# The heads' normalizer: from products with a repeated identity column to a round trip through DRAM

## The chip, the cores and the metric

The kernel runs on one core of a Trainium2 chip. The metric is device time in microseconds of one execution. The median of three runs of the kernel before is 684.15 us (682.97 to 684.3). Line numbers (L624 and so on) are those of the kernel before. TensorE is called PE, VectorE DVE, ScalarE ACT, GpSimd POOL and SyncE SP, as in the profile; SP issues nearly all DMA transfers here, ACT a few.

## The reference

2048 tokens of 640 features are normalized; one branch is a linear attention with 32 heads of 20 features and a learned feature map, the other a two-layer MLP with GELU whose output gates the first.

```python
pq = jnp.einsum("bhsd,hdf->bhsf", q, w_phi)
pk = jnp.einsum("bhsd,hdf->bhsf", k, w_phi)
phi_q = jnp.concatenate([_softmax(pq, axis=-1), _softmax(-pq, axis=-1)], axis=-1)
phi_k = jnp.concatenate([_softmax(pk, axis=-1), _softmax(-pk, axis=-1)], axis=-1)
kv = jnp.einsum("bhsf,bhsd->bhfd", phi_k, v)
z  = jnp.einsum("bhsf->bhf", phi_k)
num = jnp.einsum("bhqf,bhfd->bhqd", phi_q, kv)
den = jnp.einsum("bhqf,bhf->bhq", phi_q, z)[..., None] + 1e-6
o = num / den
...
return x + s * g      # s = o @ wo, g = silu(mlp(xn))
```

The change is about `z`: for each head, the sum of the key features over all tokens, 32 x 40 = 1280 numbers. Every token's query features are multiplied by it to get `den`.

## The kernel before

The work is in four stages.

1. Start, to about 30 us: weights are loaded, the feature map is folded into the key and query weights, tokens are normalized.
2. Projections, to about 251 us: for each of 16 token tiles of 128, keys, values and queries are projected on PE (L332). Key features are accumulated with the values into one PSUM bank `kv` by `kv_acc` (L403). The value tile carries a column of ones per head, so that each head's sum of key features falls out as one more row. The query features, not normalized yet, go to DRAM as `e_dram`, from ACT's queue (L385, L909, L911).
3. The MLP, about 251 to 555 us: twelve units, two halves of the tokens times six groups of two hidden tiles. A unit makes seven products of the first layer (`part`, L650), sums them on DVE, applies GELU on ACT (`act`, L655, L657), makes the low parts of the hidden tiles on DVE (`act_lo`, L661), and multiplies by the second layer (`down`, L679, 30 matmuls for each of the two outputs o = 0 and o = 1, each in groups of three, one and one PSUM banks); DVE adds the result to `y` (L686, L688). `down` loops over the two hidden tiles outside and over the output banks of the group inside. For o = 0 it takes the hidden tiles h11 and h21, for o = 1 h12 and h22.
4. Output, to the end: products with the state of the heads (L769, L780, L787) and with `wo` (L844), stores of the output.

In stage 3 every engine takes its instructions in the order of the code (`manual_schedule`), so the order written in the loop over units is the order of each queue, SP's too. An engine that waits holds up all that stands behind it.

Between the stages `kv_rest` (L597) copies the bank `kv` into the SBUF tile `kvr` with three ACT copies (L603); POOL clears the columns that are not used (L600, L601). In `kvr` the heads lie in groups of three: row 32e + 20 of `kvr` has the sums of group 4g + e at columns 120g to 120g + 119, for e = 0 to 3 and g = 0 to 2.

`kv_norm` (L620) spreads these four rows onto all 128 partitions. It is called once, in unit 0, after the first layer's products of that unit and ahead of its `down` (L942). For each e it takes one column of the identity, repeated 128 times, as the one operand and all of `kvr` as the other, so that each row of the product is row 32e + 20; ACT then copies the product from PSUM into the tile `zrep` (L627, L630), in the order of the heads. `zrep` is one of 23 slabs, tiles of 5120 B in each partition, that most large tiles of the kernel share; so are `eq`, `ez`, `hs`, `w1s`, `w2s`, `xhi` and `y`.

The readers of `zrep` are the sixteen products of `q_norm` (L725) on POOL: `ez` is the query features `eq` of a token tile times `zrep`. The rest of `q_norm` sums, divides and stores the normalized query features to `phi_dram`. The first `q_norm` (token tile 8) begins with unit 1, ahead of the rounding of that unit's w2 weights, whose low parts POOL makes too (L148).

On SP the order around the call is: unit 0's loads of w1 and w2 (`raw`, L154), of `xhi` and `xlo` (L699, L700) and of `eq` for tile 8 (L719); then what `kv_norm` issues, which is nothing in the kernel before; then unit 1's four loads `raw`, its `xhi`, `xlo` and its `eq` loads; then the stores of unit 0's `xhi` and `xlo` (L712, L713). The w1 weights that unit 0 loads are turned into sums and differences by POOL (L415), rounded by ACT (L426), and their low parts made by POOL (L427), within unit 0; unit 1 uses them. Those that unit 1 loads are for unit 2, and so on.

A transfer of the kind that the change brings in is used once elsewhere: `pair_stats` stores the mean and the reciprocal deviation of 256 tokens to `st_dram` (L293) and loads them back, repeated on all partitions, into `bc` (L295).

Of the kernel before, what the change touches and what calls it, by code (L numbers as in the profile page):

```python
# [8 lines left out]
F32 = mybir.dt.float32  # L9
F32R = mybir.dt.float32r  # L10
AF = mybir.ActivationFunctionType
# [3 lines left out]
S, D, H, DH, F = 2048, 640, 32, 20, 1536  # L15
P = 128
# [30 lines left out]
def hedgehog_gated_mlp_kernel(ctx: ExitStack, tc: tile.TileContext, x, xt_in, wqk, bd, wv, wo, w1, b1, w2, b2, out_t):  # L47
    nc = tc.nc
# [4 lines left out]
    dram = ctx.enter_context(tc.tile_pool(name="dram", bufs=1, space=bass.MemoryType.DRAM))  # L53
# [27 lines left out]
    def slab(dt, name, shape=(P, 2, D)):  # L81
        return slabs.tile(list(shape), dt, tag="S", name=name)
# [7 lines left out]
    def bankB(name="pB"):  # L90
        return pools["B"].tile([P, 512], F32, tag="B", name=name)
# [4 lines left out]
    xd_dram = dram.tile([P, 9, 2, CW], F32, name="xd_dram")  # L96
    w1_dram = dram.tile([NG, P, 2, 2048], F32, name="w1_dram")
    g_dram = dram.tile([KC, P, 2, CW], F32, name="g_dram")
    st_dram = dram.tile([NT // 2, 2, P, 2], F32, name="st_dram")

    ident = const.tile([P, P], F32, name="ident")
# [495 lines left out]
    def kv_rest():  # L597
        kv_acc(NT - 1, phis.pop(NT - 1), vs.pop(NT - 1))
        kvr = const.tile([P, 360], F32, name="kvr")
        nc.gpsimd.memset(kvr[64:96, 320:360], 0.0)  # L600
        nc.gpsimd.memset(kvr[96:, 240:360], 0.0)  # L601
        for p, a, b in ((P, 0, 240), (96, 240, 320), (64, 320, 360)):
            nc.scalar.activation(kvr[:p, a:b], kvp[0][:p, a:b], AF.Copy)  # L603
        return kvr


    def kv_state(kvr):
# [8 lines left out]
        for r in range(3):  # L616
            nc.vector.tensor_tensor(bdl[:80, 40 * r:40 * r + 40].rearrange("p (h d) -> p h d", d=20),
                                    ps[:80, None, 320:340].to_broadcast([80, 2, 20]),
                                    mask[:80, :2, None].to_broadcast([80, 2, 20]), op=OP.mult)
    def kv_norm(kvr):  # L620
        zf = slab(F32, "zrep")[:].rearrange("p a b -> p (a b)")
        for e, n in enumerate((360, 360, 320, 240)):
            ps = bankB()
            nc.tensor.matmul(ps[:, :n], ident[:, 32 * e + 20:32 * e + 21].to_broadcast([P, P]), kvr[:, :n],  # L624
                             start=True, stop=True)
            m = n // 120
            nc.scalar.activation(zf[:, :960].rearrange("p (g r) -> p g r", r=480)[:, :, 120 * e:120 * e + 120],  # L627
                                 ps[:, :240].rearrange("p (g r) -> p g r", r=120), AF.Copy)
            if n > 240:
                nc.scalar.activation(zf[:, 960 + 120 * e:720 + 120 * e + n], ps[:, 240:n], AF.Copy)  # L630
        return zf


# [220 lines left out]
    zf, none = None, iter(())  # L854
# [6 lines left out]
    kvr = kv_rest()  # L861
# [8 lines left out]
    for unit in range(units):  # L870
        h, g = divmod(unit, NG)
# [69 lines left out]
        if unit == 0:  # L941
            zf = kv_norm(kvr)  # L942
# [146 lines left out]
```

## Time and profile before

| What | Value |
|---|---|
| Median of three runs | 684.15 us (682.97 to 684.3) |
| Profiled execution: span from the first to the last instruction | 681.1 us |
| Granted TensorE clock over the span (mean) | 1.000 |
| PE busy, stretch of units 0 (251.5 to 279.5 us) | 28.0 us of 28.0 |
| DVE, ACT, POOL busy in the same stretch | 19.2, 16.2, 19.7 us |
| L624, products of `kv_norm` on PE | 8 matmuls, 263.6 to 265.9 us |
| L627 and L630, copies of `kv_norm` on ACT | 7, the first at 267.13, the last at 268.30 us |
| First reading of `zrep` on POOL | 279.08 us |

The page gives the span of the profiled execution and not its whole time; the runs are timed apart from it. PE's busy time is a sum of modelled spans; its rate is better read from how many matmuls fall into a stretch of the chain. Rows of the timeline have the start, the duration, the engine, the line and operation, the tiles (out<-in) and, in brackets, how long the engine was idle before and what ended that. A q after the engine's name is its queue: SPq rows are transfers issued by SP, with the time that the issue took, waits within a group of them included. A row of waits has who waited, for what, the sum in us, how often, and the longest.

### The profile page before, as it was taken

The page shows a single profiled execution, that of the slowest core. Times are in us where ns is not written, and L with a number is a line of the kernel's source. Part 1 is how long each engine was busy: PE and PEld are TensorE (multiplying, and loading weights), DVE is VectorE, ACT ScalarE, POOL GpSimd, SP SyncE. Part 2 cuts the span into 40 slices and gives each one's busy share as a digit, 9 for nine tenths or more (in the row PEclk, how much of TensorE's full clock was granted, in tenths as well). Part 3 has the DMA queues.
Part 4 walks back from the last instruction along what each step waited for, and adds up shares of the span by engine and source line. Part 5 has one row for each costly group of instructions (what it writes and reads, how often), then busy time and mean ns, then how long its engine had stood idle before and what let it go on. Part 6 is the DMA issues. An engine that isn't in the chain of part 4 may idle for free.

```text
span 681.1 us, 11991 instructions
## 1 busy us (share of the span) xinstructions
PE 676.4 (99%) x4727; PEld 592.0 (87%) x4727; DVE 454.8 (67%) x729; ACT 253.0 (37%) x400; POOL 382.2 (56%) x351
## 2 busy tenths in 40 slices
PE   9999999999999999999999999999999999999998
PEld 9999999999999998888888888888888887777876
DVE  5786665887876466586978784576876655774232
ACT  3523214333223337144254247533133254425440
POOL 3653254757767375857978952726446640783221
PEclk9999999999999999999999999999999999999999
DMA  8820144633451333329688696476363491888423
GB/s 330 311 80 1 11 142 100 227 93 137 69 200 60 115 138 135 117 88 348 209 273 278 237 426 280 129 259 224 139 216 137 151 398 47 321 296 291 150 94 109
DMA packets 73966, 125.42 MB, mean 184 GB/s; under 512 B 5822, under 2 KB 42686, under 8 KB 73014
## 3 DMA queue, kind: packets, MB, share of 16 engines
q1 hardware_dynamic: 71606, 114.17, 49.3%
q10 hardware_dynamic: 2304, 10.49, 4.4%
q8 instruction: 37, 0.61, 0.4%
q14 instruction: 19, 0.16, 0.1%
HBM read 79.54 MB, written 45.10 MB: 183 GB/s over the span
## 4 chain that ended last, share of the span: by engine, by line
PE 96%; DVE 1%; POOL 1%; issue 1%; ACT 0%; POOLq 0%
PE pA L332 30%; PE pB L679 24%; PE pB L650 22%; PE pB L844 11%; PE pB L780 3%; PE pB L769 2%; PE kv L403 2%; PE pA L173 1%; POOL wv L148 1%; PE pA L466 1%; PE pA L318 1%; PE pB L787 1%; DVE st L197 0%; DVE wk L184 0%; PE pB L624 0%
## 5 line engine op out<-in xcount | busy, mean ns | idle before, releaser
L679 PE MATMUL pB<-hs,w2s 128*128 128x512 f32 x720 | 167.1, 390 | 0.0
L679 PEld LDWEIGHTS pB<-hs,w2s 128*128 128x128 f32 x720 | 134.6, 188 | 29.4 <-PE pB L780 0.8
L650 PE MATMUL pB<-xp,w1s 128*128 128x512 f32 x324 | 81.4, 390 | 0.0
L650 PE MATMUL pB<-xd,w1s 128*128 128x512 f32 x324 | 79.3, 389 | 0.0
L358 ACT ACTIVATE e<-e 128x1280 f32<-128x1280 f32 x32 | 40.7, 1272 | 90.1 <-POOL e L353 89.5
L844 PE MATMUL pB<-oT,wo 128*128 128x512 f32 (+2 forms) x315 | 73.9, 386 | 0.0
L688 DVE TENSOR_TENSOR y<-pB,y 128x512 f32<-128x512 f32 x100 | 63.9, 680 | 12.4 <-PE pB L679 12.2
L650 PEld LDWEIGHTS pB<-xp,w1s 128*128 128x128 f32 x324 | 60.7, 188 | 12.9 <-DVE pB L925 0.4
L650 PEld LDWEIGHTS pB<-xd,w1s 128*128 128x128 f32 x324 | 60.8, 188 | 12.6
L844 PEld LDWEIGHTS pB<-oT,wo 128*128 128x128 f32 x315 | 57.1, 188 | 14.2 <-ACT ph L772 1.2
L371 POOL TENSOR_TENSOR e<-e,rc 128x1280 f32<-128x1280 f32 x16 | 39.0, 2438 | 48.8 <-DVE rc L391 48.4
L371 POOL TENSOR_TENSOR eq<-eq,rc 128x1280 f32<-128x1280 f32 x16 | 37.9, 2369 | 50.2 <-DVE rc L738 50.2
L353 POOL TENSOR_TENSOR e<-nr,e 128x640 f32<-128x640 f32 x32 | 45.5, 1424 | 30.1 <-DVE nr L352 27.7
L332 PE MATMUL pA<-wv,xp 128*128 128x320 f32 x384 | 60.7, 311 | 0.3 <-POOL wv L148 0.3
L655 ACT ACTIVATE pB<-pB,b1t 128x512 f32<-128x512 f32 x48 | 31.8, 662 | 77.2 <-DVE pB L925 27.6
L332 PE MATMUL pA<-wk,xp 128*128 128x320 f32 x384 | 59.9, 311 | 0.0
L332 PE MATMUL pA<-wq,xp 128*128 128x320 f32 x384 | 59.0, 309 | 0.0
L332 PEld LDWEIGHTS pA<-wv,xp 128*128 128x128 f32 x384 | 56.9, 188 | 0.6 <-POOL wv L148 0.5
L332 PEld LDWEIGHTS pA<-wq,xp 128*128 128x128 f32 x384 | 56.9, 188 | 0.1
L332 PEld LDWEIGHTS pA<-wk,xp 128*128 128x128 f32 x384 | 56.8, 188 | 0.1
L725 POOL TENSOR_TENSOR ez<-eq,zrep 128x1280 f32<-128x1280 f32 x16 | 47.3, 2959 | 0.2 <-PE pB L780 0.2
L427 POOL TENSOR_TENSOR w1s<-raw,w1s 128x640 fp32r<-128x640 f32 (+1 forms) x18 | 25.7, 1428 | 36.4 <-ACT w1s L426 29.2
(145 smaller groups left out, 1053.3 us busy)
## 6 DMA issues: line engine op xcount, KB each, us to landing
raw<-in_w_dram SPq DMA_DIRECT2D x42, 320.0 KB, 4.7
e_dram<-e ACTq DMA_DIRECT2D x16, 640.0 KB, 3.8
eq<-e_dram SPq DMA_DIRECT2D x16, 640.0 KB, 6.6
phi_dram<-eq SPq DMA_DIRECT2D x16, 640.0 KB, 3.5
phi<-phi_dram SPq DMA_DIRECT2D x16, 640.0 KB, 9.0
xt<-in_x_dram SPq DMA_DIRECT2D x16, 320.0 KB, 5.7
xres<-in_xt_dram SPq DMA_DIRECT2D x20, 256.0 KB, 4.3
out_dram<-xres SPq DMA_DIRECT2D x18, 256.0 KB, 3.0
```

The source lines that it names most:

```text
L332: nc.tensor.matmul(ps[:, hf, :HALF], stat_x(q, o, k, a), ws[k][:, b, hf * HALF:(hf + 1) * HALF], start=n == 0, stop=n == 3 * KC - 1)
L353: nc.gpsimd.tensor_tensor(e5[:, :, :, 1, :], nr[:, :, :, None].to_broadcast([P, 2, 16, DH]), e5[:, :, :, 0, :], op=OP.subtract)
L358: nc.scalar.activation(ef, ef, AF.Exp)
L371: nc.gpsimd.tensor_tensor(e3, e3, rc[:, :, None].to_broadcast([P, 64, DH]), op=OP.mult)
L427: nc.gpsimd.tensor_tensor(sl[:, 1, :n], src, sl[:, 0, :n].bitcast(F32), op=OP.subtract)
L650: nc.tensor.matmul(bank[ch][:], tl[:, a, off + wo_:off + wo_ + P], mov(blk, b), start=new and n == 0, stop=n == len(mms) - 1, skip_group_c ...
L655: nc.scalar.activation(ps, ps, AF.Gelu_apprx_tanh, bias=b1t[:, f:f + 1])
L679: nc.tensor.matmul(ps[:], ws[i][:, b, d * P:(d + 1) * P], hs[o][i][:, a, :], start=i == n == 0, stop=(i, n) == (GF - 1, 2), skip_group_che ...
L688: nc.vector.tensor_tensor(y, ps[:], y, op=OP.add)
L725: nc.gpsimd.tensor_tensor(zv, ef, zf, op=OP.mult)
L780: nc.tensor.matmul(po[64 * e:64 * e + 64, :256], bdk[:n, 2 * j + e, :], ph[:n, e * 256:(e + 1) * 256], start=True, stop=True)
L844: nc.tensor.matmul(ps[:, mv], w, o[:, mv], start=n == 0, stop=n == 15, skip_group_check=True)
```

## The change

The four products and the seven ACT copies go. In their place SP issues six transfers: five stores from `kvr` to a new DRAM tensor `z_dram` and one load that repeats its 1280 numbers on all 128 partitions into the slab. Four stores take one row of `kvr` each, as pieces of 120 numbers that go to every fourth place of 120 in `z_dram`; the fifth takes the 80 numbers of the last group. The load reads what the stores write, so it waits for all five. The place of the call, the readers and the form of `zrep` stay as they are.

```diff
+    z_dram = dram.tile([1440], F32, name="z_dram")
...
     def kv_norm(kvr):
+        zv = z_dram.rearrange("(g e r) -> e g r", e=4, r=120)
+        for e, m in enumerate((3, 3, 2, 2)):
+            nc.sync.dma_start(zv[e:e + 1, :m], kvr[32 * e + 20:32 * e + 21, :120 * m].rearrange("p (g r) -> p g r", r=120))
+        nc.sync.dma_start(z_dram[1200:2 * D].unsqueeze(0), kvr[84:85, 240:320])
         zf = slab(F32, "zrep")[:].rearrange("p a b -> p (a b)")
-        for e, n in enumerate((360, 360, 320, 240)):
-            ps = bankB()
-            nc.tensor.matmul(ps[:, :n], ident[:, 32 * e + 20:32 * e + 21].to_broadcast([P, P]), kvr[:, :n],
-                             start=True, stop=True)
-            m = n // 120
-            nc.scalar.activation(zf[:, :960].rearrange("p (g r) -> p g r", r=480)[:, :, 120 * e:120 * e + 120],
-                                 ps[:, :240].rearrange("p (g r) -> p g r", r=120), AF.Copy)
-            if n > 240:
-                nc.scalar.activation(zf[:, 960 + 120 * e:720 + 120 * e + n], ps[:, 240:n], AF.Copy)
+        nc.sync.dma_start(zf, z_dram[:2 * D].partition_broadcast(P))
         return zf
```

## The prediction

> **What bounds the kernel now.** I read the page first, for the busy shares and the chain that ended last, then what TensorE waited for over the whole run, then its chain in the stretch around the change.
>
> ```profile
> span 681.1 us, 11991 instructions
> PE 676.4 (99%) x4727; PEld 592.0 (87%) x4727; DVE 454.8 (67%) x729; ACT 253.0 (37%) x400; POOL 382.2 (56%) x351
> PE 96%; DVE 1%; POOL 1%; issue 1%; ACT 0%; POOLq 0%
> ```
>
> ```profile
> PE pA L466 <- PEq L1079: 0.8, 1, 0.8
> PE pA L332 <- POOL wv L148: 0.3, 1, 0.3
> PE pA L318 <- DVE xt L213: 0.2, 1, 0.2
> ```
>
> ```profile
> 251.49 12.26 PE pB L650 x54
> 263.75 2.15 PE pB L624 x8
> 265.90 13.63 PE pB L679 x60
> 279.54 12.24 PE pB L650 x54
> 291.78 13.60 PE pB L679 x60
> ```
>
> The reader is to see three things. The list of PE's waits holds three entries, 1.3 us together, all at lines of the first phase, and the chain is 96% PE: every microsecond of matmul on it is a microsecond of time. In the chain one piece begins where the other ends (251.49 + 12.26 = 263.75, + 2.15 = 265.90). And the pace is that of streaming, not of waiting: 13.60/60 and 12.24/54 are both 0.227 us per matmul, in a unit with the changed code before it and in one without. The eight matmuls of L624 (four calls, two hardware passes each) sit in this row with 2.15 us and nothing beside them.
>
> **Removed: four products, 2.15 us of PE.** Without them the first matmul of the second layer (L679) could start at 263.75. Whether it may is a question of its inputs. The first nine matmuls use the hidden tile h11 alone, the next nine h21, because the loop over the two weight tiles is outside that over the three outputs.
>
> ```profile
> 262.36 0.68 DVE L661 TENSOR_TENSOR hs<-pB,hs 128x512 fp32r<-128x512 f32 x1
> ...
> 264.62 0.69 DVE L661 TENSOR_TENSOR hs<-pB,hs 128x512 fp32r<-128x512 f32 x1 [0.49 <-ACT hs L657]
> ```
>
> The code makes the low parts in the order h11, h22, h21, so these are the first and the third: h11's is there at 263.04, h21's at 264.62 + 0.69 = 265.31. Nine matmuls from 263.75 take 9 x 0.227 = 2.04 us, so h21 is asked for at 265.79: 0.48 us after it is there. The last hidden tile, h12, is read only by the other half of the tokens, 30 matmuls (6.8 us) further on. The four PSUM banks that the products took fall away too, and unit 1 goes from L650 to L679 without a gap (291.78) with no products between. So the whole 2.15 us leaves the chain at this point.
>
> **Removed: seven ACT copies.**
>
> ```profile
> 267.13 0.37 ACT L627 ACTIVATE zrep<-pB 128x240 f32<-128x240 f32 x1
> 268.55 0.81 ACT L426 ACTIVATE w1s<-raw 128x640 fp32r<-128x640 f32 x1
> ```
>
> From 267.13 to 268.55, 1.42 us, they hold up the rounding of unit 1's weights. ACT is waited for by POOL there (below), so POOL's run begins 1.42 us sooner, while PE comes 2.15 us sooner: POOL loses 0.73 us of its lead.
>
> **Added: five stores, one load and their waits, all on SP.** The order on SP is the order of the code; the new six stand behind eq (t = 8) and ahead of unit 1's four raw loads.
>
> ```profile
> 236.25 2.04 SPq L719 DMA_DIRECT2D eq<-e_dram  x1
> 247.33 11.64 SPq L154 DMA_DIRECT2D raw<-in_w_dram  x4
> 272.09 0.53 SPq L699 DMA_DIRECT2D xhi<-xp_dram  x1
> 295.53 0.57 SPq L712 DMA_DIRECT2D xd_dram<-xhi  x1
> 296.93 0.54 SPq L713 DMA_DIRECT2D xd_dram<-xlo  x1
> ```
>
> ```profile
> 251.72 0.55 ACT L603 ACTIVATE kvr<-kv 128x240 f32<-128x240 f32 x3
> 255.94 0.19 POOL L601 MEMSET kvr<- 32x120 f32 x1
> ```
>
> SP is free at 236.25 + 2.04 = 238.3 and must wait for kvr: until ACT's copies end at 252.27, or until POOL's clearing ends at 256.13 if the stores are held for that as well (they do not read those columns). I take the later one. The trace has no store of one partition's row; the nearest is the store of the layer norm's statistics with the repeating load that waits for it:
>
> ```profile
> 177.90 0.37 SPq L293 DMA_DIRECT2D st_dram<-pst  x1
> 182.62 0.34 SPq L295 DMA_DIRECT2D bc<-st_dram  x1
> bc<-st_dram SPq DMA_DIRECT2D x4, 256.0 KB, 5.7
> eq<-e_dram SPq DMA_DIRECT2D x16, 640.0 KB, 6.6
> ```
>
> An issue is 0.37 us and the dependent load follows 182.62 - 177.90 - 0.37 = 4.35 us later. Five issues (1.85) and one such round trip: SP issues the load at 256.13 + 1.85 + 4.35 = 262.3 (258.5 by the early end). The load repeats one row of 5120 B onto 128 partitions, 640 KB. From below it costs 5.7 us, the 256 KB that L295 repeats in the same way; from above 2.5 times that for 2.5 times the bytes, 14.3. I take 6.6, the load with the same bytes and the same rows in SBUF, which differs only in that its source rows are not one row. So the normalizer lands at 268.9, and between 264.2 and 276.6.
>
> **Who waits for it.** The first reader is POOL's product ez (L725) of unit 1, and behind it on POOL stand the low halves of unit 1's w2 tiles (L148) that PE needs at 291.78.
>
> ```profile
> 269.44 1.58 POOL L427 TENSOR_TENSOR w1s<-raw,w1s 128x640 fp32r<-128x640 f32 x1 [8.01 <-ACT w1s L426]
> 279.08 2.96 POOL L725 TENSOR_TENSOR ez<-eq,zrep 128x1280 f32<-128x1280 f32 x1
> 282.00 3.08 POOL L148 TENSOR_TENSOR w2s<-raw,w2s 128x640 fp32r<-128x640 f32 x2
> 287.78 0.74 POOL L415 TENSOR_TENSOR st<-raw 128x256 f32<-128x256 f32 x1 [2.70 <-PE pB L650]
> ```
>
> POOL works without a break from 269.44 into ez, so it comes to ez at 279.08 - 1.42 = 277.66. Up to there a landing costs nothing, and both bounds lie before it. PE is hit only later: it wants the first low half after one matmul of L679, at 291.78 - 2.15 + 0.23 = 289.86; ez (2.96) and half of 3.08 go before, so a landing after 289.86 - 4.50 = **285.36** stalls PE, one for one. Margin 16.5 us on my value, 8.8 on the worst. The cover is POOL's own run; without it the whole wait would be paid.
>
> Behind the new waits on SP stand the four raw loads. They go out by about 264 instead of 247.33 to 259. POOL reads the first at L415, at 287.78 - 2.15 = 285.6, and itself waited for PE there, not for a load. Four loads of 320 KB are two of 640 KB, 2 x 6.6 = 13.2 us even one after the other: they are in by 282.1 if the normalizer lands at 268.9, by 289.8 if at 276.6. Even then POOL makes unit 2's forms in four steps like L415 and some four like L427, 4 x 0.74 + 4 x 1.58 = 9.3 us, by 299.1, and PE wants them at 291.78 + 13.60 - 2.15 = 303.2. I cost it at nothing. xhi, which follows, was held until 272.09 by a slab that PE's L679 frees:
>
> ```profile
> SPq L699 <- PE pB L679: 9.0, 1, 9.0
> SPq L713 <- DVE xlo L710: 0.7, 1, 0.7
> ```
>
> so SP has time to spare up to there. The normalizer's own tile takes its place in the pool of slabs some 5 us earlier (262.3 against 267.13); if it had to wait as xhi did, until 272.09, it would land at 278.7 (286.4 by the upper bound): a loss of 0 to 1.0 us.
>
> **The sum.** -2.15 (PE) + 0 (ACT, POOL, SP, the load) = -2.15 us; the span 681.1 becomes 678.95. The page gives no time of the whole execution beside its span; the median of the runs, 684.15, is 3.05 above it, and I keep that difference: **682.0 us**, 0.31% less. From L679 of unit 0 on, PE waits for nothing in the list above, so the gain travels to the end.
>
> **The rivals.**
> *The late normalizer (slower).* If each of the five stores waits for the one before, because their targets in DRAM are interleaved, SP pays 5 x 4.72 (177.90 to 182.62) = 23.6 us and issues the load at 279.7; it lands at 286.3 by the 640 KB row, 285.4 and 294.0 by the bounds. PE stalls 0.05 to 8.7 us: 682.0 to 690.6, with 685 in the region of a landing at 288.4. It decides from a landing of 285.36 on, and from 287.5 the kernel is slower than before. Against it: L712 and L713 above write interleaved stretches of one DRAM tensor, and the second goes out 1.40 us after the first and was held only 0.7 us, by DVE, though such a store takes longer to land:
>
> ```profile
> xd_dram<-xhi SPq DMA_DIRECT2D x4, 576.0 KB, 3.5
> ```
>
> For it: the views of z are three-level and different in the fifth store, and a single-partition store is nowhere in this trace. The Trainium skill, page "DMA: Bandwidth & Descriptors", section "Anatomy of one DMA", puts a transfer at about 2.0 us plus its bytes at 436 GB/s and lays the fixed part to the confirmation of the write; by that even the stores one after the other would cost some 10 us and the load 3.5, an estimate that lands before 277.66 and costs nothing. The 4.35 us of the row above is twice that page's figure, so the rows count.
>
> *No gain at this place.* PE has its 2.15 us less of products but waits for the hidden tiles: if h21's low part were needed from the first matmul, L679 would start at 265.31 instead of 265.90, a gain of 0.59, 683.6 us. For it: DVE's third L661 ends only 1.56 us after 263.75. Against it: the order of the loop, and the 0.48 us of lead. The same size would come from slabs given out in another order, so that a tile of a later unit waits as xhi does; every such wait lies on SP now, and none is on PE.
>
> **How the numbers follow.** The forecast 72%, no gain 12%, late normalizer 16%. Under 0.2%, 1.37 us, a measurement of this kernel cannot be told from no change (its three runs lie 1.33 apart). The forecast is faster; no gain is "same"; of the late landings, spread evenly over 285.4 to 294.0, a tenth is faster (stall under 0.78), three tenths same (under 3.52), six tenths slower. Faster 0.72 + 0.01 = 0.73, same 0.12 + 0.05 = 0.17, slower 0.10. The range: from the lowest run before less 2.15 and a little for the runs, 682.97 - 2.15 - 0.2 = 680.6, up to 685.0, which takes in all of "no gain" and the late landings up to 288.4; the forecast's own is 680.8 to 682.8.
>
> **What would show it.** Right: L679 of unit 0 follows L650 with no gap and no row of L624; PE's waits still sum to 1.3 us; ez of unit 1 starts near 277.7 and is released by POOL's own order; the load of z goes out at 258 to 263 and lands before 277; the five stores leave within 2.5 us; ACT's L426 starts at 267.1. Wrong: a wait of POOL for the load at ez, a wait of PE for POOL's L148 at the second layer of unit 1, stores about 4.7 us apart on SP, PE waiting for DVE's L661 at 263.75, or a new PE wait after 305 that eats the 2.15.

## The result and the profile after

The changed kernel takes 681.8 us in the median of eight runs, beside 683.65 us of the kernel before: a ratio of 0.9973, with a 95% interval of 0.9963 to 0.9983. A second set of runs gave 681.13 beside 683.23 us, 0.9971 (0.996 to 0.9981). The forecast was 682.0. The profiled execution has a span of 679.2 us and a time of 680.95, near the lower end of the eight (680.72 to 683.57).

The chain that ended last, around unit 0, of the changed kernel (start, duration, piece; the lines of the MLP are now L647 and L676):

```profile
251.64 12.27 PE pB L647 x54
263.90 13.60 PE pB L676 x60
277.50 12.24 PE pB L647 x54
289.74 13.60 PE pB L676 x60
303.34 12.24 PE pB L647 x54
```

From the first matmul of the MLP to the first of the second layer there are now 12.26 us, where there were 14.41: the 2.15 us of the products are out and nothing stands in their place. They stay out: the last long piece of PE, 112 matmuls with `wo`, begins at 652.68 instead of 654.71, and the MLP itself had begun 0.15 us later here, which makes 2.18 us between the two points.

The issues of SP around the call:

```profile
252.45 2.76 SPq L624 DMA_DIRECT2D z_dram<-kvr  x4
255.26 0.42 SPq L625 DMA_DIRECT2D z_dram<-kvr  x1
257.64 0.35 SPq L627 DMA_DIRECT2D zrep<-z_dram  x1
258.04 1.86 SPq L155 DMA_DIRECT2D raw<-in_w_dram  x4
270.05 0.58 SPq L696 DMA_DIRECT2D xhi<-xp_dram  x1
```

SP's waits in this stretch, and the landing of the repeating load in the list of DMA issues:

```profile
SPq L624 <- ACT kvr L604: 14.3, 1, 14.3
SPq L627 <- DMA z_dram<-kvr: 1.8, 2, 1.3
```

```profile
zrep<-z_dram SPq DMA_DIRECT2D x1, 640.0 KB, 5.1
```

SP waited 14.3 us for ACT's copies into `kvr`, not for POOL's clearing: the first store went out at 252.45, and POOL began to clear only at 255.93. The five stores left within 255.26 + 0.42 - 252.45 = 3.23 us, none held by another, and the load went out 1.96 us after the last of them. It landed at 262.7 (257.64 + 5.1), with no wait for a free slab, and the four weight loads behind it were out by 259.9.

POOL in the same kernel, from the low parts of unit 1's weights on:

```profile
268.14 1.58 POOL L428 TENSOR_TENSOR w1s<-raw,w1s 128x640 fp32r<-128x640 f32 x1 [6.56 <-ACT w1s L427]
277.30 0.46 POOL L268 TENSOR_TENSOR xlo<-xhi 128x128 f32<-128x128 f32 x1
277.73 2.96 POOL L722 TENSOR_TENSOR ez<-eq,zrep 128x1280 f32<-128x1280 f32 x1
280.63 3.10 POOL L149 TENSOR_TENSOR w2s<-raw,w2s 128x640 fp32r<-128x640 f32 x2
```

The row of ez has no idle time in brackets: POOL came to it at 277.73 from its own work, fifteen microseconds after the normalizer was there.

Three signs that the prediction named did not come as named. The load went out at 257.64, before 258 to 263; the five stores took 3.23 us and not at most 2.5; and PE's waits sum to 1.9 us here and to 1.5 in the profile of the second set, not to 1.3. What is new among these waits is 0.5 and 0.4 us for a weight load at the start and, here alone, 0.3 us for DVE in the output stage, in either case far from the change; the kernel before with its hidden tiles exchanged (below) has such waits too, 0.6 and 0.2 us.

### The profile page after: what moved, and what is told of

Read it like the earlier page. It is cut to its first block, busy times and chain, and to the rows that moved or that the text cites. A ratio compares the mean times of both kernels' runs of the same rounds, so it can differ in the third digit from the quotient of the medians.

```text
span 679.2 us, 11970 instructions
## 1 busy us (share of the span) xinstructions
PE 673.8 (99%) x4719; PEld 590.4 (87%) x4719; DVE 453.1 (67%) x729; ACT 251.2 (37%) x393; POOL 381.9 (56%) x351
## 4 chain that ended last, share of the span: by engine, by line
PE 92%; DMA 6%; POOL 1%; DVE 0%; issue 0%; SPq 0%; DVEq 0%; POOLq 0%
PE pA L333 30%; PE pB L676 23%; PE pB L647 20%; PE pB L841 11%; PE pB L777 3%; PE kv L404 2%; PE pB L766 2%; DMA raw<-in_wo_dram 2%; DMA phi<-phi_dram 1%; PE pA L174 1%; DMA raw<-in_wv_dram 1%; DMA folds<-in_wqk_dram 1%; DMA xt<-in_x_dram 1%; PE pB L784 1%; POOL wv L149 0%; PE pA L319 0%
## 5 line engine op out<-in xcount | busy, mean ns | idle before, releaser
L676 PE MATMUL pB<-hs,w2s 128*128 128x512 f32 x720 | 166.9, 390 | 0.0
L676 PEld LDWEIGHTS pB<-hs,w2s 128*128 128x128 f32 x720 | 134.7, 188 | 29.3 <-PE pB L777 0.8
L647 PE MATMUL pB<-xp,w1s 128*128 128x512 f32 x324 | 81.3, 389 | 0.0
L647 PE MATMUL pB<-xd,w1s 128*128 128x512 f32 x324 | 79.3, 389 | 0.0
L647 PEld LDWEIGHTS pB<-xd,w1s 128*128 128x128 f32 x324 | 60.8, 188 | 12.6
L647 PEld LDWEIGHTS pB<-xp,w1s 128*128 128x128 f32 x324 | 60.7, 188 | 12.6 <-DVE pB L922 0.2
```

The lines of the kernel that those rows point to most:

```text
L647: nc.tensor.matmul(bank[ch][:], tl[:, a, off + wo_:off + wo_ + P], mov(blk, b), start=new and n == 0, stop=n == len(mms) - 1, skip_group_c ...
L676: nc.tensor.matmul(ps[:], ws[i][:, b, d * P:(d + 1) * P], hs[o][i][:, a, :], start=i == n == 0, stop=(i, n) == (GF - 1, 2), skip_group_che ...
```

## The experiments

Ratios are to the kernel before, run beside each; the changed kernel stands at 0.9973 and 0.9971. The theory: the gain is the products' 2.15 us on an unbroken chain of PE, PE's inputs were just early enough to let it all out, and the round trip through DRAM is hidden under POOL's run with some twenty microseconds to spare. The rivals: the seven ACT copies made the gain, or part of it; SP's new waits cost something that the gain outweighs.

**The products back, their result unused.**

```diff
         zf = slab(F32, "zrep")[:].rearrange("p a b -> p (a b)")
+        for e, n in enumerate((360, 360, 320, 240)):
+            ps = bankB()
+            nc.tensor.matmul(ps[:, :n], ident[:, 32 * e + 20:32 * e + 21].to_broadcast([P, P]), kvr[:, :n],
+                             start=True, stop=True)
         nc.sync.dma_start(zf, z_dram[:2 * D].partition_broadcast(P))
```

> The changed kernel with the four products put back at their old place (their result is copied nowhere; the normalizer still comes through DRAM). If the gain is PE's 2.15 us of products on an unbroken chain, the products cost 2.15 us again: within 0.3 us of the kernel before, ratio 0.999 to 1.001, span 681.0 to 681.5, and the second layer of unit 0 starts 14.4 us after the first layer's first matmul there. If the gain came from the seven ACT copies, the time stays at the changed kernel's, ratio 0.997.

Measured: 1.0004 (0.9995 to 1.0013), span 681.3. The chain of this kernel:

```profile
251.71 12.26 PE pB L651 x54
263.97 2.15 PE pB L629 x8
266.12 13.63 PE pB L680 x60
```

The same 2.15 us as before, 14.41 from L651 to L680, and the whole gain is gone, though the seven copies are still away and the normalizer still comes through DRAM. The products' place on PE is the gain.

**Copies back on ACT, seven and four.**

```diff
+    junk = const.tile([P, 240], F32, name="junk")
...
+        for n in (240, 120, 240, 120, 240, 80, 240):     # second run: (240, 120, 240, 120)
+            nc.scalar.activation(junk[:, :n], kvr[:, :n], AF.Copy)
         nc.sync.dma_start(zf, z_dram[:2 * D].partition_broadcast(P))
```

> The changed kernel with seven ACT copies of the old sizes at their old place (from kvr into a tile that nobody reads). If the copies were off the path, the time is the changed kernel's, ratio 0.997, with the second layer still starting where the first ends; POOL comes to its first ez some 1.4 us later (279.1 instead of 277.7). If the copies made the gain, the ratio is 0.999 or above.

> The changed kernel with four ACT copies at the old place, one after the other, some 1.5 us in all (the seven of the kernel before took 1.42 because they overlapped; the seven of the last such run took 2.68). If the copies were off the path, the time is the changed kernel's, ratio 0.9965 to 0.998, with no wait of PE in units 0 to 3. If they bought part of the gain, ratio 0.998 or above and a wait of PE for DVE in unit 3 as in the run with 2.68 us of copies.

Seven copies gave 0.9984 (0.9976 to 0.9993), four gave 0.9975 (0.9966 to 0.9984). The first lies between the two expectations. The copies were longer than meant: 2.68 us for seven, 0.38 each, one after the other, where the old seven had overlapped. All of them write one tile here, which is the likely reason. These are the rows of ACT, first of the run with seven, then of that with four:

```profile
267.52 2.68 ACT L629 ACTIVATE junk<-kvr 128x240 f32<-128x240 f32 x7
```

```profile
267.57 1.50 ACT L629 ACTIVATE junk<-kvr 128x240 f32<-128x240 f32 x4
```

With 1.50 us, about what the old copies took (1.42), the time is that of the changed kernel, and PE has no wait in the MLP. POOL came to ez at 279.38, 27.5 us after the start of the MLP, as in the kernel before (27.6), so what the old copies did to POOL is back and the gain stays. In the profiled execution, the slowest of that kernel's eleven, PE waited 0.9 us for DVE in the output stage, where the changed kernel's profile has 0.3; that wait was not followed up. With 2.68 us POOL came to ez at 280.5 instead of the expected 279.1, and PE is unbroken through units 0 to 2 too, but it has one wait in unit 3 (waits of PE of that run):

```profile
PE pB L650 <- DVE pB L925: 0.7, 1, 0.7
```

0.7 us is about what separates this run from the changed kernel (0.0011 of 683, 0.75 us), though the two intervals overlap, so that the runs alone do not tell them apart. So copies of the old size were off the path and did not make the gain. What leads from 1.2 us more of copies in unit 0 to a wait in unit 3 was not settled: POOL in unit 2 stood 5.6 us for a store of the w1 forms there, 1.8 more than in the changed kernel, and DVE followed POOL; that this began with the copies was not tried.

**A longer round trip.** The numbers go through further DRAM tensors, each copy waiting for the one before; 4, 12 and 18 hops.

```diff
+    z_hops = [dram.tile([1440], F32, name=f"z_hop{i}") for i in range(4)]     # 12, 18
...
-        nc.sync.dma_start(zf, z_dram[:2 * D].partition_broadcast(P))
+        src = z_dram
+        for dst in z_hops:
+            nc.sync.dma_start(dst[:2 * D].unsqueeze(0), src[:2 * D].unsqueeze(0))
+            src = dst
+        nc.sync.dma_start(zf, src[:2 * D].partition_broadcast(P))
```

> The changed kernel with four more round trips: the 1280 numbers go through four further DRAM tensors, each copy waiting for the one before, all on SP ahead of the repeating load. A hop costs some 2.4 us (issue 0.42 and the 1.96 us from the last store to the load), so the load goes out at 267 instead of 257.6 and lands at 272 (bounds 270 to 282 with 2 to 4.7 us a hop), before POOL comes to ez at 277.7. If the wait is hidden as reckoned, the time is the changed kernel's: ratio 0.997. If SP is on the path, the ten microseconds show: ratio above 1.005.

> Twelve further round trips: the load goes out at about 286 and lands at 291 (bounds 287 to 319). PE wants the low half of unit 1's first w2 tile at 289.97, ez and that half take 4.5 us of POOL before, so from a landing of 285.5 on PE stalls one for one: 5.8 us for a landing at 291.3, ratio 1.0055, with the wait at the second layer of unit 1 and POOL waiting for the load at ez. If the landing is another, the stall is the landing less 285.5. If the cover is longer than reckoned, no stall; if the loads queued behind on SP are what hurts, the gap of PE lies in unit 2, not in unit 1.

> Eighteen further round trips, at the 2.05 us a hop that the run with twelve showed: the load goes out at 257.8 + 18 x 2.05 = 294.7 and lands, 4.3 us later, at 299.0. If PE loses one for one from a landing of 285.8 on (the run with twelve: landing 286.7, 0.9 by this rule, 1.4 measured), it loses 13.2 to 13.7 us in unit 1, net of the 2.15 gained 11 to 11.6 us: ratio 1.016 to 1.017. If other work gives part of it back, or the loads queued behind on SP add to it, the loss before unit 2 is the same and the end differs: ratio below 1.014 or above 1.019.

Four hops: 0.9968 (0.9955 to 0.998). The load went out at 266.03, 8.4 us later than in the changed kernel, with everything behind it on SP, and the time is the changed kernel's. Waits of this size on SP cost nothing here.

Twelve hops: 0.9988 (0.9979 to 0.9998). A hop took 2.05 us and not 2.4, so the load went out at 282.41 and landed at 286.7; the expected 1.0055 had been worked out from a landing at 291.3. POOL's timeline of this kernel, then PE's waits, then its chain that ended last:

```profile
286.86 2.95 POOL L727 TENSOR_TENSOR ez<-eq,zrep 128x1280 f32<-128x1280 f32 x1 [8.80 <-DMA zrep<-z_hop]
289.77 3.07 POOL L150 TENSOR_TENSOR w2s<-raw,w2s 128x640 fp32r<-128x640 f32 x2
```

```profile
PE pB L681 <- POOL w2s L150: 1.1, 1, 1.1
```

```profile
282.41 4.30 DMA zrep<-z_hop
...
289.77 1.56 POOL w2s L150
...
291.37 13.67 PE pB L681 x59
305.05 12.24 PE pB L652 x54
```

The chain leaves PE here and runs through the load and POOL. ez waited 8.80 us for the load. POOL took 7.7 of these 8.8 us out of its lead and PE stood 1.1 us, for the low half of the first w2 tile, as the prediction had named it. Unit 2 begins 27.24 us after unit 1 (277.81 to 305.05) instead of 25.84 (277.50 to 303.34): a loss of 1.40 against 0.9 by the rule that counts from a landing of 285.8 (285.36 moved by the later start of the MLP, 251.95 instead of 251.49). The wait itself fits the rule if it is counted from the start of ez, 286.86 - 285.8 = 1.1; the other 0.3 us are in the 59 matmuls behind it, 13.67 us instead of 59 x 0.2267 = 13.37, and why those were slower was not settled.

Eighteen hops: 1.0181 (1.0167 to 1.0195), slower than before and a little above the 1.016 to 1.017 that was expected; the last section shows where the rest comes from. PE's wait and the stretch after it (waits of PE, then its timeline, whose window ends after 24 of the 59 matmuls that follow):

```profile
PE pB L681 <- POOL w2s L150: 12.8, 1, 12.8
```

```profile
289.83 0.39 PE L681 MATMUL pB<-hs,w2s 128*128 128x512 f32 x1
303.05 7.28 PE L681 MATMUL pB<-hs,w2s 128*128 128x512 f32 x24 [12.83 <-POOL w2s L150]
```

ez began at 298.62, so the rule gives 298.6 - 285.8 = 12.8 us, and 12.83 was measured. The wait is one for one from the start of ez. The trace has no landing of the repeating load in this run, and it names a weight load issued behind it as what ended the wait of ez; ez reads only `eq` and `zrep`, and it began 4.56 us after the repeating load went out (294.06), in keeping with the 4.3 us of the run with twelve.

**The hidden tile h21 first.** In unit 0, for the first output alone, the loop over the two hidden tiles is turned round; once in the changed kernel, once in the kernel before.

```diff
-    def down(g, ws, hs, o, mid=None):
+    def down(g, ws, hs, o, mid=None, order=range(GF)):
...
-            for i in range(GF):
+            for i in order:
...
-        dn = down(g, w2g, hs, 0)
+        dn = down(g, w2g, hs, 0, order=(1, 0) if unit == 0 else range(GF))
```

> The changed kernel, in unit 0 with the second hidden tile (h21) taken first in the first output of the second layer. In the changed kernel the high part of h21 is there at 264.78 and its low part at 265.50, PE comes at 263.90. If the order of that loop is what lets the whole 2.15 us out, PE now stands 0.9 us at its first matmul and 0.2 to 0.4 us more at its third, 1.2 us in all: ratio 0.9985 to 0.9995, span 680.3 to 680.6. If PE's inputs are not close behind it, nothing changes: ratio 0.997.

> The same exchange of hidden tiles in the kernel before. There the products keep PE until 265.90, and h21 is there at 265.31, so the exchange costs nothing: ratio 1.000, no gap behind the products. If the exchange is dear in itself, it costs here what it costs in the changed kernel.

In the changed kernel: 0.9993 (0.9985 to 1.0002), span 680.5. In the kernel before: 1.0002 (0.9993 to 1.0011). PE's timeline in the first, where a bracket shows the stop, and the chain in the second, where there is none:

```profile
261.36 2.20 PE L647 MATMUL pB<-xp,w1s 128*128 128x512 f32 x9
264.46 14.17 PE L676 MATMUL pB<-hs,w2s 128*128 128x512 f32 x60 [0.91 <-ACT hs L654]
```

```profile
251.14 12.26 PE pB L650 x54
263.40 2.15 PE pB L624 x8
265.55 13.63 PE pB L679 x60
```

0.91 us at the first matmul, for the high part that ACT makes, and 14.17 - 13.60 = 0.57 more within the 60, where PE's weight load also waited 0.4 us for DVE's low part: 1.48 us, a little over the 1.2 expected, and 0.0020 of 683, 1.4 us, in the runs. In the kernel before the same exchange is free, since the products kept PE until h21 was there. So most of the 2.15 us would have turned into a wait for GELU's output if the loop had been the other way round.

**The changed kernel again.**

> The changed kernel once more, beside the other runs: ratio 0.9965 to 0.998; PE gets to the second layer of unit 0 at the end of the first (12.26 us after the first matmul of the MLP, not 14.41).

0.9971 (0.996 to 0.9981); the second layer of unit 0 follows 12.26 us after the MLP's first matmul, as expected.

## Why the prediction was right

- *The 2.15 us of PE.* Right: the products alone, put back, cost 2.15 in the chain and the whole of the gain in the runs.
- *Inputs at 263.75.* Right, by the loop's order, as the exchange of hidden tiles shows. DVE's third L658 of the changed kernel ends at 264.81 + 0.69 = 265.50, and PE asks for h21 at 263.90 + 2.04 = 265.94, a lead of 0.44 against the predicted 0.48:

```profile
264.81 0.69 DVE L658 TENSOR_TENSOR hs<-pB,hs 128x512 fp32r<-128x512 f32 x1 [0.49 <-ACT hs L654]
```

- *ACT's copies.* Right in effect: POOL came to ez at 277.73 (predicted 277.66), and copies of the same length put back cost nothing.
- *SP.* Right that it is hidden, with four terms mis-sized. The stores began at 252.45, released by ACT's copies, where the later of two readings, POOL's clearing at 256.13, had been taken: 3.7 us. The five issues took 3.23 us and not 1.85: 1.4 us the other way. The wait from the last store to the load was 1.96 us and not 4.35. The load landed in 5.1 us and not 6.6, under the lower bound of 5.7 too. Together the normalizer was there at 262.7, 6.2 us before the 268.9 that had been taken and before the whole range of 264.2 to 276.6. No harm came of it because three of the four errors were on the safe side.
- *The row for the round trip.* The 4.35 us came from one of four round trips of the statistics in the kernel before, and not from a typical one. These are their waits together, and the landing of the store:

```profile
SPq L295 <- DMA st_dram<-pst: 15.0, 4, 4.7
st_dram<-pst SPq DMA_DIRECT2D x4, 2.0 KB, 3.4
```

Singly the four waits are 3.0, 3.0, 4.7 and 4.3 us, while the store landed 3.3 to 3.4 us after the start of its issue each time. So some 1.3 of the 2.4 us of error lay in the choice of the instance, and what lengthened the last two waits was not settled. The rest, 3.0 against 1.96, is between that store of 128 partitions of pairs and these stores of one partition; that the shape makes this difference was not tried.

- *The point from which it costs.* Right: 285.36 was predicted, 285.8 with the later start of the MLP in the run with eighteen hops, and PE then waited 12.83 us for 12.8.
- *The late normalizer, 16%.* Its mechanism was right, as the runs with twelve and eighteen hops show, and its price was not. No store was held by another; and at 2.05 us a hop, stores one after the other would have added about 8 us (4 x 2.05), while the run with four hops added 8.4 at no cost. At these prices a chance of 16% was too much. The Trainium skill, page "DMA: Bandwidth & Descriptors", section "Anatomy of one DMA", gives about 2.0 us for the fixed part of a transfer on GpSimd's path. The hops here were issued by SP; they took 2.26, 2.05 and 2.01 us each in the runs with four, twelve and eighteen, close to that figure, which the prediction had set aside for the row of 4.35.
- *No gain at this place, 12%.* Its way of losing is real, as the exchange of hidden tiles shows; it took the other order of the loop.

That the time of 682.0 came out so close (681.8) is in part luck. It starts from the median of three runs, 684.15, and the eight runs of the same kernel have 683.65, from which 2.15 less would be 681.5. The 3.05 us between span and time is no property of the kernel either: it sets a median beside the span of another run, and in each run of the changed kernel the time is 1.7 to 1.8 us above its own span.

The span fell by 1.9 us (681.1 to 679.2) and the medians by 1.85 and 2.10, for 2.15 predicted; the start of the MLP alone varies between 251.1 and 252.0 in these profiles, so the rest of the difference says nothing. Counted inside the run, from the start of the MLP to the last long piece, the gain is the 2.18 us given above.

## What to carry to other kernels

Where one engine's chain has no gaps, even a small group of instructions is worth its length in the chain if the inputs of what follows are there, and a round trip through DRAM can take its place if its reader comes late enough; work out the landing, the reader's arrival and the point from which the bound engine waits, and keep the three apart. What stood on the bound engine may have covered a wait of its own: look at what the next instruction reads, and when that is ready. For the price of a transfer look at every instance of the row from which it is taken, and not only at the nearest in time: here four of them lay between 3.0 and 4.7 us.

## What the runs showed of the hardware

In the run with eighteen hops the long stop of PE cost more than its length. The granted clock fell while PE stood, and it stayed low for a while after (stretches of that kernel: start and end, length, the busy times of PE, PEld, DVE, ACT and POOL with their counts, PE's granted clock, DMA share, GB/s):

```profile
289.80:296.00 6.20, 0.42 (x2) 0.00 (x0) 2.73 (x4) 2.52 (x4) 0.00 (x0) 0.74 0.17 51
300.00:303.00 3.00, 0.00 (x0) 0.00 (x0) 0.00 (x0) 0.28 (x1) 3.00 (x3) 0.50 1.08 363
303.00:306.00 3.00, 2.95 (x7) 2.38 (x8) 0.00 (x0) 0.00 (x0) 2.92 (x4) 0.50 1.14 369
306.00:309.00 3.00, 3.00 (x13) 2.45 (x13) 1.59 (x3) 1.27 (x2) 3.00 (x4) 0.94 1.09 350
```

At clock 0.50 seven matmuls begin in 3 us instead of thirteen (3 / 0.2267). The 59 matmuls after the stop took 15.22 us, 1.85 more than 59 x 0.2267 = 13.37 (0.2267 is 13.60/60). With this the sum comes out: 12.83 + 1.85 - 2.15 = 12.5 us, and the medians are 12.2 apart (695.42 and 683.23). The 1.1 us stop with twelve hops left the clock at 1.00.

An estimate from these rows, if the clock has only the two levels 1.00 and 0.50: a mean of 0.74 over the first 6.20 us puts the fall at 292.8, some 2.6 us after the last matmul before the stop had ended (289.83 + 0.39), and a mean of 0.94 over the last row puts the return at 306.4, 3.3 us after PE had begun again. Half speed for 3.3 us loses some 1.65 of the 1.85 us; the 0.2 left over is near the 0.3 us behind the short stop, where the clock did not fall. The Trainium skill describes this on "TensorE: Matmul & The Clock Gate", section "What's actually happening": half clock after an idle window of about 3.4 us, full clock again after a busy one of that length. The trace agrees with the half clock and with the time of the return; the fall came sooner than 3.4 us after the last matmul.
